# A recomputed order table for the same operations, and other forms for some filling matmuls

## The chip, the cores and the metric

The kernel runs on one core of one Trainium2 chip. The metric is the device time of the run in microseconds, lower is better. Times before and after come from runs on a chip; the profile is one further execution of the same program, taken by the hardware profiler.

## What is computed

The reference runs two layers one after the other on an input of 4 batches, 6272 time steps and 256 channels. The first is a gated recurrence over time, the second a gated long convolution over time, with a projection before and after it. Cut to what matters:

```python
sig = 1 / (1 + exp(-f_logit))
f = lower_bound + (1 - lower_bound) * sig
for t in range(S):                      # S = 6272
    h = f[:, t] * h + (1 - f[:, t]) * x[:, t]
    y[:, t] = h
proj = y @ w_proj                       # 256 -> 768
x1, x2, x3 = split(proj, 3)             # 256 channels each
x2c = irfft(rfft(x2, axis=time) * rfft(filter_fft, axis=time))
out = (x1 * x2c * x3) @ w_out           # 256 -> 256
```

Inputs and output are fp32.

## The kernel before

The kernel works through the four batches. Each goes through these stages, and the names are those by which the operations are called in the code (`kind`), in the trace lines and in the prediction.

- **Recurrence** (`hgrn`): 13 chunks of 512 time steps (the last of 128). SP loads `f_logit` into FL and `x` into XT, three buffers each (L301). ACT takes the sigmoid of FL (`sig`, L304), POOL multiplies XT by it (`u`, L306), PE transposes both in 128x128 fp32 pieces (`sT`, `uT`, L313), ACT or DVE forms the forget gate (`f`, L327 or L329), and DVE runs the scan (`scan`, L335) into the fp16 tile HA. A copy of the first 3072 steps (`wrap`, ACT or POOL) follows.
- **x2 projection** (`P`, L662): 13 groups on PE, twelve of four blocks and one short one of a single block. Each group is copied into the tile X2 by ACT or DVE (`x2`); the short copy is 128x256, the others 128x1024. All of them must be done before F1.
- **Spectrum**: 16 units. `F1` (L675) and its copy `A`; `F2` (L720); the product with the filter's spectrum Hu, two per unit, always on DVE (`prod`, L733); `slot` on POOL (L725); `I2` (L743) and its copy `Th`. SP loads Hu (`H`, L710) into three buffers in turn; such a load waits for the products that last read its buffer.
- **Gate** (`x13`, L362): x1 and x3, copied by ACT or DVE (`xs`), multiplied on POOL (`z`, L378).
- **Output** (`phase_o`): `I1` (L776), the gating product `y` on DVE (L782), `proj` (L794), the copy `o` into one of three buffers osb by ACT or DVE, and the store by SP (L804).

Stages of neighbouring batches overlap: the recurrence of the next batch runs beside the spectrum and output of the current one.

Before batch 0 the filter is transformed once (`prepare`): 13 blocks are loaded (L568), cast to fp32r by ACT, DVE or POOL (`fr`) into two buffers in turn, rotated on PE (`rot`, L579), copied (`f2`), and then transformed by `FF1` (L604, copy `afs`) and `FF2` (L622, copy `hw`, stores `hst`, L630). Between the rotations PE runs 32 blocks of filling matmuls (`warm`, L550) whose results nobody reads. Tables of sines and cosines are made on the way.

The order of all this is not found at run time. Every operation is first entered into a list with the engines that may run it. The long text ORDER then holds one entry of three characters for each of the 2438 operations: its number, the engine that it runs on, and the PSUM bank that it uses. The program is emitted in exactly this order, so that each engine, and SP's queue of DMA issues too, works through its own part of the table in sequence; what an operation must wait for on other engines is done with semaphores. Decoding is short:

```python
word = a * 4096 + b * 64 + c
yield word // 64, self.ENGINES[word // 8 % 8], word % 8
```

Of the kernel before, what the change touches and what calls it, by code (L numbers as in the profile page):

```python
# [10 lines left out]
F32R = mybir.dt.float32r  # L11
# [10 lines left out]
S = 6272  # L22
D = 256
M = 128
Q = 49
# [33 lines left out]
class Plan:  # L59
# [58 lines left out]
    "BLgAAYBBgAOYABIA6QA8gACIBGgAsRBQgBagAwSA7YBVgAPIBkgAqTBfgAtUBpgA2VBCYAeWERgA9ABDQBugA+SBEAAgXBHYAfUBAKAQABzg"  # L118
    "ArVBFIBMYA3WBIUARIB4gAmXBRAAVYBNQAYYAnWBJEESgA5XA/CBSWBPAApSBbYBOAADgAyTBUGA0SAzTBWABcQEfgAvSBTOBeABlYBXSBdA"
    "AUIAkWEggBgIBKEAxXBYCA4QBZCAdREtgASABhWETAAjUBqYBmQEugAoVBnIBvYAuSBjOAiTAFgBrUBiGATIBwSBoABsMB0YEVWBtEB5IAcX"  # L120
    "BxCAWIAEYB6QByCB1UEUYB8IB7AAlXB3EB2MAhSEXOB/QEhACKSCAICBUCIWCCEEiYEWQCJGEaRCLCCTUEcJE7gEvACNWEYICESCDYCOGCMY"
    "EbREwYCUEEjQEdJE8gEkWElAEoXCFCCaUEmOFJgEpQAZYCbEExRFKgEqHCRSCQgCcUCGgErICSCClWAHACVYCWSEzBCdMEyQE9ACmOCeYE2R"
    "E0IE3UE4BFXgE+YE/VFYgCXCCjWE5MCsQCkGCYgCfSFLACPgFBNCoWCHgCnYC1UCtACpOFMYCgCFAQFERFCIC2EFFWFlgFGBFNXCZgC3SB9Y"
    "FmgFHOFPHFOUFZACuQC4KFSVDJWFQMFUFFxgFTSCrgAIAFbTFygCvAFVKC6UChgFdDCwYCigCxQC5YC7EFaYDHSCyIDKGC+UFnADAWC/MDSQ"
    "AJADIKFcUDBGFgVFeMDCYDMSFoYFiFF9gDDWAKAAbVDEODTADQUALAFhQFzADLYDRMFpRF+gDbWFjIFrBCqgF0YDZUAMAFqRDaEFtQFsJDNC"
    "FuUGJgF1VGKgDcGDUYDVSF3NCzgDdYDeWDWCFvIF2RFwMF/ADkSF5VDlCF4JF6QGAYGVgF7FA1UGWgDtSDfGF8IDiUDuCGBRDrWDjEAaYGDJ"
    "GCSGLAGFTDmYGEKD0UE1AGhgGMYGGQGHDGNRDsOGigDnSGPJC0gC8gDwWD1EGIIDvYGXAGORFRYD2UGQJGRQGYYD3EGtgEeAD9UGTIC9gFDA"
    "GSRD+EGZQGUJGugD/UD4YGbADGgFWYDFgGjAGaQDXgEAMAGgGdRGcIGeUGkYGfBGlVDoCGgMD5QGnFEGSDqgDxODPgGvAEBYGmUDYgGwYEHC"
    "DOgGpVMvgGoMAXYEISE6YGrFDzgGqWM9gFIYEJCGxXGyVGsOJsUD6ADygEKYFfYEPSANAEsYGzPECQEQCG0NEZYELWFkYG1VEMGG2SJtTEnY"
    "G3NG4KJxVB+YEDAENgHCWG5gNLgJuEM+gHGQJvDD7gEEgJzFJwYHOSDpgHHIHDGEFgHEUM/AMwgHPKHAWEOgHFEHKQHBOJySD8gJ2THLIJ0C"  # L130
    "G8UMxAG6WNAYG9EHIQJ4DHSUHJIHQSHTEJ1YNNAG+UHegHRKG7GHMQG/EJ3SHNIHlgJ7TJ5CDggJ8WDhgJ6YMzXJ9LJ+GNMgHUUM1HHWQJ/Y"
    "HVEKASHXIHYWKBTMyYHZGHfUKDLHmQKCCHiMKFWHsgHaSKHGHhMKGXKEYM0VKIHKKWHoIHbCKLUKJYM4XKMGHcSM2NKPQNZgKNEHzgKQWKRA"
    "KOYM5UHdKKSGNBVM6HHpIKUQKTYH8SKWANCWM7MIEgNDFH6QHgYHnYH9CNOYKVXH7INGVKXHKZUNngNIFHjSNagNEOKbEHtQKYYHkCH0UHvI"
    "KaXNbAKeWHuYHwIHqSKcHKgGKfQH1YHrCH2MKdYH+WILgKjRH/GIASKhIKkUKlBH3MHxWKiYIBCIFQHyOKmEICSNHVNpAKnYIDKIgWNogKoU"
    "NJNISgIhGKpSKtTKqEIIIH4WKrCKuVH5GKsYIHIKyUKzSKvDIMWKwFIGYK0MIZgM8YIiQK1CIOOINYK3TKxYIjANPVNQUIPONRFK4SIJQK6C"
    "NSMIqgK5DITVIUYNqYIKANUXIWNNVSNWHN1gNdTIkQNXKNfDIaWK2YIlAIQTIVNImQNcYIRDK8SIdOIxgInAIXTIcOK9VIYDLBXK7YIoQK/F"
    "IrTI4gIpIK+CLCWIuLN3AIbYLGVLAYIeQLDHItLLHSLEGNeULJCLFYJGWI/gNgMLIFNiTN2gIfANjSIsYLKYNrVJHGNkLIyQNlKNtFJITNKY"
    "IvWIzYJJDI1ILLVIwGLMSLQTI0ILNFI5WLOCJKUI7OLSDJQgLPYNsRJLEODgLRQOEgNuJI2SN4YLTANwWI3CI8OJAUM3ALVQNyGNxRJDMJXg"
    "LUYLWSLaTLYCNzJJMWI6YLXALbVJNGLZYN5SJCMN6QN7CJOWLfRJPOLcDJegN+ULhBN8IOPgI9SLdFOQgOAEJRWLeYJYQI+CJUOLgVOFAJSY"
    "LkUJBYJESJTONYAOGYN/XLiFJbIOHWJlgLmEObgJFCJVUOcgJaIOJGJfRJZYJWELjYLlTJiJLpWLnDLqQN0AJcULoYJhJLsAOITLrGJnYSJS"  # L140
    "JdEJgYOBPNmYJmQORALtYOLWJpIJjUONGOngOSYOMXSLCJoISKWJkEOogOTRSMGSOSOKLOdAJqUOUQOOPOVBOeYOXWOYTJrEOfROWIO0gOZG"
    "LuUOzgSQCLzWLvMOhBSPQOpAOgSL0OOjRLwUNvAOqYO/gSRAOaLL4WLxEOkQL5OOlBOrTLygNTYL1UOmIL6WL2EOiKL9QL7GL3gMCUPAgL+I"
    "OsSOtDOvWO1AMDMOwXPLgL/QOxGL8gO2YOuKP7gO3TMAAMEUOyPO5DMBgMHQOCAMMSMIIMFEO4WO7XPBAMGgMNKMJUVMgO9HPMgPCYO8QO6O"
    "PNAPDRMKEMRSO+INhAMWWMLgMOUN9AQJgNFYMSKPFBPEQMPEPHRPGIMTSPJBMQgQCgMbUMXOMUCPIRPOYVOAMcMPPQMYSPRAPQWPKJPTXMZC"
    "MdUPUQPSOVQSPVHVpgPWIMgWMagVSKPrQVagMeEMhOMVgPZSMfgPsIVNgMlUVbgPnWPaKPbQPoGMmMPlSPjWPmCPhUPkOPtSPiEPcIPXWPuC"
    "PpUPYGPvQMqSPqEPwIPfWPdQPgGMiUPeIVcAMnWMjEMrKSNYPxQMoGPzSPyIP3UVPYP0CP1WP4MSTQP2GP8RSVAQDWP+JSSYP5TSUVSYQP6L"
    "SWFSZRSaAP/JSXYQXTSbBSdVQYDQZQQGOQQgQEYSeSP9YQaAQATQFOSiXSfFQLYScYSjQSgCQKVQhgQBDVogQHRShYQNNSlASkHSnTSoUQIB"
    "QMNQSYSmYQRWSpDQiQSqEQTOQogQOSSrYMpgSsVQUOQPCStUSxWSvESuNQVSSzGQkISwYSyXQWCQbUS2WQlIS0HVRQQcES1YQdSVTIS3XQeC"
    "VVRVdYQpUVXJV2gS4GQfSS7QQvgS5HQsMQ2gVWWS9AS8RQgKTAXS6YS+BVeQVYOQ/SQqYTBVQjYRACS/YVfRQrMVjWTCHMsSVgIVlGRHgTDF"
    "V3gTFUMtKVqAWEgQ9WTEYTHMQwSVhJQ+GTGQVUYQmUTIATKWTJYQnEQzKQtQTMGRBUQyKQuAQ4YQ3WVrYRCETLTQ6OROgRDQVkSREAVsUQ5O"  # L150
    "WFgQxYTPVTNDQ0QTRFVmKTOYRVgRIWVuETQTQ1ARLOQ7UTSDRjQQ8ERFSRGKRkARWURKORPSRQYTTYWGATUXRlQRRKRcgTWHRJYTVWWHYRmA"
    "TZXRSKVtSTbHRMQRtgTaXRNARZMVxTRXYTXGRTQRYMTcHRdVRUATdYTeXRgNR0gVzDRaQWSgTYYV4ATfURfNTjTRbATkWReYV5YVvKR7gThE"
    "RnQMugTlDRuUTmGRhSRxMRoAToWTgHRpQRwMVyVTiYRqAV6XWTgRiKTpUSCgV8HTnYRrQTqGRsIR1STrEV0NR8WWUATtQTsYTuRR3KTvATyU"
    "V1YTwBV7VT0ERvYTzQR4KR2YTxYV/RT1AWASWggWBBV9NRyTWhgT2YMkgR5QRzDR+OT3VSEYWVYT4TT5FWCKWIUT6DT8WWKEWJVR/OT+GSDS"
    "R6AT9UR9YT7YSGKUBWVZAUCXT/ESAQWLNUDGWNTUEHWOUSBAUFYWsgSFKUGWWtgWiAWWXUAYWXVWPLWbQWYHSHRWQMW4gWjYUIGUHTSIBamX"
    "WZNanWUJDWcUWdAWkRW5gUKYapGWeMWlSWmBWoTVnYaoHarQXEgWnKWpVVwYatAUQWXFgWqDUaQUROWuAULSasUWvYUMKUSWauEW6AWwUWrN"
    "UNSWyEUTGWDYUbIWxVWRYW0UUOCUkWUUgW7YWzNUVQW2EUPgW1SUWIXGAXQgW8TXRgUcUW+DWMYW3KXHYW9QXARW/IUXSXCBXcgUdEXBRUlO"
    "XIQUYCUfUXDJUuWV+AUZgUmSXKAXdgUgMUegXSAXJRUvOXMQXTYUhUXOAXogXLJUpWUiEXNQUqOXeAXURXpgXVUUjgXPIXYVXWBUrWXfYUnC"
    "XXMXZRXaFUogXgQUsGdpgUzSXbJU4UXiAUtgU9WU0KWaAUwQXqAXrYU1SUxAU5MViAXhQUygU+OU2CXkRdqgVCUXjIXmBXlWdrAXsXXtSXwT"
    "XnOU6QeFgXuHU3gWfAd4gXvKU7AU/WVDMXyDXxSVHQVAGdtTXzKYAUdsYdvLVBgeGgX+WYBEd3gYmgX2SX/OYYgYfgYKUVIIX3KYIWavYYEQ"  # L160
    "YJGaqYX6SYLEawWX7KYFAaxXX8UeHAYMQYGSYNAX9EX4QYHKYCUX5AX0SYDMayGa1QX1Ca2Ra3IduWazHa4JYOUa0YYQSdwOYPEYUQa6XYVA"
    "a5YYRKYSUa7WYTEa/Qa9OYZRbBAYWTY0VYbJa8HbAQa+YY1FbEXYXLbFRbCAYgVYcJbHBbDYYnTbGHY2QYiNYtgbJSYaYY3AbIYbKXYjNbOV"
    "bLCdyQYhYbMHYdRd0IY+gbQFYkWYeBYqLYoYbNYbPVYlGY4QYpLbTSbRFYuWbVCbSYbUUZFgY5AYwObYVYvYY6SbWEYxOYrQbaFbXYY7CbZW"
    "YsIY/UZMgdxYbbGeTgY8SbdXd5AY9KYyQZBMbfHZaSZHYYzAZAYbeWbcYZCMbiXZbCZGQZNUZTgbgGZIIZDSbkHZJIbjWZECZOYbhYdzXblG"
    "ZcSZPMd7QbmYZdCbnRZQMboWbpBZKSd6Yd9Ad1PZrgZUUZLCZkgbsRbqGZWMZeSbuBZgWbrYZfCZRQZXMbtUZVYZSAbxSZhOZygbyTbvEd8V"
# [24 lines left out]
def kernel(  # L190
# [193 lines left out]
    def prepare(tmp):  # L384
# [162 lines left out]
        def warm(e, p):  # L547
            half = iden[:].bitcast(F16)
            for i in range(4):
                nc.tensor.matmul(PS[:, p, 0:256], half[:, 0:128], half, start=True, stop=True)  # L550
        for i in range(WARM):
            op("warm", {"PE": 0.435}, warm, r=["iden"], take=1)
# [313 lines left out]
```

## Time and profile before

| | us |
|---|---|
| Median of 3 runs | 487.26 |
| Lowest and highest of them | 486.27, 487.69 |
| Profiled execution | 488.11 |
| Its span, first to last instruction | 486.3 |
| PE busy in the span | 467.5 |
| DVE busy | 425.1 |
| ACT busy | 417.5 |
| POOL busy | 295.0 |

The profiled execution lies 0.85 us above the median, so a difference that is worked out in its trace is applied to the median. Busy times of PE are modelled at the ends of matmuls, which overlap in the pipeline: a row of several matmuls is read by the distance from one start to the next, not by the mean of one. The first P of each batch starts at 79.8, 183.1, 292.0 and 396.8 us.

### The profile page before, as it was taken

To read this page: it belongs to the slowest core of one execution; us is meant where nothing else is said; L and a number is where in the kernel's file an instruction comes from. 1 tells how busy PE (TensorE), PEld (TensorE's weight loads), DVE (VectorE), ACT (ScalarE), POOL (GpSimd) and SP (SyncE) were. 2 spreads that over 40 slices of the span, in tenths; PEclk is the share of its full clock that TensorE was granted. 3 is DMA by queue.
4 is the path that set the end of the run, shared out by engine and by line. 5 is a ranking of instruction groups with operands and counts; after the bars stand their busy time and mean duration, and the time that the engine had idled before them with its cause. 6 is when DMAs were issued, how large, how long until landed. Compare 5 with 4: busy or idle time off the path is not lost.

```text
span 486.3 us, 13200 instructions
## 1 busy us (share of the span) xinstructions
PE 467.5 (96%) x5257; PEld 374.3 (77%) x5257; DVE 425.1 (87%) x454; ACT 417.5 (86%) x613; POOL 295.0 (61%) x305
## 2 busy tenths in 40 slices
PE   7999999999999999999999999999999999999895
PEld 6878878777777989777778889766788997676684
DVE  8769897699999997798999985999989978999873
ACT  4989989899999885989999887999998975999654
POOL 7677686686869430686888523667797432655600
PEclk9999999999999999999999999999999999999998
DMA  8979888775678898179667999256788870365167
GB/s 329 402 249 343 288 288 266 275 233 165 182 237 260 284 356 306 40 218 261 197 207 260 343 315 324 54 166 219 253 273 295 344 273 2 107 218 157 52 250 282
DMA packets 41725, 116.39 MB, mean 239 GB/s; under 512 B 4384, under 2 KB 6304, under 8 KB 41664
## 3 DMA queue, kind: packets, MB, share of 16 engines
q1 hardware_dynamic: 41664, 115.56, 70.9%
q8 instruction: 41, 0.67, 0.5%
q14 instruction: 20, 0.16, 0.1%
HBM read 84.54 MB, written 31.00 MB: 238 GB/s over the span
## 4 chain that ended last, share of the span: by engine, by line
PE 73%; ACT 10%; DMA 6%; DVE 4%; issue 4%; POOL 2%; SPq 0%; ACTq 0%; DVEq 0%; POOLq 0%
PE PS L362 15%; PE PS L313 15%; PE PS L743 8%; PE PS L794 7%; PE PS L662 7%; PE PS L720 6%; PE PS L675 6%; DMA out_dram<-osb 5%; PE PS L776 3%; PE PS L604 3%; ACT f L273 2%; ACT osb L275 2%; DVE X L278 1%; ACT Th L273 1%; PE PS L622 1%
## 5 line engine op out<-in xcount | busy, mean ns | idle before, releaser
L378 POOL TENSOR_TENSOR zt<-x1s,x3s 128x490 f16<-128x490 f32 (+1 forms) x104 | 125.6, 1216 | 74.9 <-ACT x3s L273 31.7
L733 DVE TENSOR_TENSOR PP<-PS,Hu 98x1008 f16<-98x1008 f32 x128 | 147.4, 1198 | 5.3 <-PE PS L720 2.3
L306 POOL TENSOR_TENSOR XT<-XT,FL 128x1024 f32<-128x1024 f32 (+1 forms) x52 | 116.9, 2249 | 55.9 <-ACT FL L304 24.1
L335 DVE TENSOR_TENSOR_SCAN HA<-fTs,HA,PS 128x512 f16<-128x512 f32 (+1 forms) x96 | 113.8, 1204 | 7.1 <-PE PS L313 3.9
L362 PE MATMUL PS<-HA,W 128*128 128x490 f16 (+1 forms) x416 | 107.5, 368 | 0.0
L782 DVE TENSOR_TENSOR ys<-PS,zt 128x1024 fp32r<-128x1024 f32 (+1 forms) x52 | 58.8, 1151 | 7.0 <-PE PS L776 4.8
L313 PE MATMUL PS<-iden,XT 128*128 128x128 f32 x392 | 61.2, 276 | 2.8 <-POOL XT L306 1.1
L327 ACT ACTIVATE fTs<-PS,nomc 128x512 f32<-128x512 f32 (+1 forms) x87 | 58.7, 676 | 5.7 <-PE PS L313 3.5
L275 ACT ACTIVATE osb<-PS 128x1024 f32<-128x1024 f32 (+1 forms) x49 | 48.0, 988 | 16.9 <-PE PS L794 10.2
L313 PE MATMUL PS<-iden,FL 128*128 128x128 f32 x392 | 60.6, 275 | 0.5 <-DVE PP L733 0.4
L273 ACT CAST HA<-PS 128x1024 f16<-128x1024 f32 x56 | 56.7, 1024 | 4.6 <-PE PS L675 4.3
L743 PEld LDWEIGHTS <-PP 98*128 98x128 f16 x1024 | 50.0, 98 | 12.2 <-issue 3.2
L275 ACT ACTIVATE x1s<-PS 128x490 f32<-128x490 f32 (+1 forms) x97 | 57.2, 594 | 2.5 <-PE PS L362 0.7
L794 PE MATMUL PS<-Wo,ys 128*128 128x256 f32 x392 | 57.6, 291 | 1.4 <-ACT osb L275 0.7
L273 ACT COPY x3s<-PS 128x490 f32<-128x490 f32 (+1 forms) x94 | 53.7, 577 | 5.9 <-PE PS L362 4.6
L304 ACT ACTIVATE FL<-FL 128x1024 f32<-128x1024 f32 (+1 forms) x52 | 53.7, 1033 | 0.5 <-DMA FL<-in_f_logit_dram 0.4
L313 PEld LDWEIGHTS PS<-iden,XT 128*128 128x128 f32 x392 | 44.6, 140 | 11.2 <-issue 3.0
L794 PEld LDWEIGHTS PS<-Wo,ys 128*128 128x128 f32 x392 | 49.3, 188 | 4.7 <-ACT osb L275 1.7
L362 PEld LDWEIGHTS <-W 128*128 128x128 f16 x416 | 34.6, 98 | 23.3 <-issue 6.4
L743 PE MATMUL PS<-VA,PP 98*128 98x98 f16 x512 | 52.1, 207 | 0.4 <-DVE PP L733 0.2
L273 ACT CAST Th<-PS 128x784 f16<-128x784 f32 x60 | 49.8, 831 | 2.9 <-PE PS L743 2.3
L743 PE MATMUL PS<-VB,PP 98*128 98x98 f16 x512 | 51.9, 207 | 0.0
(111 smaller groups left out, 692.0 us busy)
## 6 DMA issues: line engine op xcount, KB each, us to landing
Hu<-H SPq DMA_DIRECT2D x64, 392.0 KB
FL<-in_f_logit_dram SPq DMA_DIRECT2D x48, 512.0 KB
XT<-in_x_dram SPq DMA_DIRECT2D x48, 512.0 KB
out_dram<-osb SPq DMA_DIRECT2D x48, 512.0 KB
X<-in_moe_filter_fft_dram SPq DMA_DIRECT2D x9, 512.0 KB
H<-Hu SPq DMA_DIRECT2D x16, 196.0 KB
H<-Hu SPq DMA_DIRECT2D x16, 128.0 KB
Hu<-in_moe_filter_fft_dram SPq DMA_DIRECT2D x2, 512.0 KB
```

Of the source, the lines that this page charges most:

```text
L273: nc.scalar.copy(dst, src)
L275: nc.scalar.activation(dst, src, AF.Copy, scale=scale)
L306: op("u", {"POOL": 0.1 + 0.553 * nb}, lambda e, xt=xt, ft=ft: nc.gpsimd.tensor_tensor(xt, xt, ft, op=AOP.mult), r=[("ft", k)], w=[("xt", k)])
L313: nc.tensor.transpose(PS[:, p, j:128 * nb:nb], src[:, j, cols], iden[:])
L327: nc.scalar.activation(fT, PS[:, p, 0:n], AF.Identity, scale=by, bias=1.0)
L335: nc.vector.tensor_tensor_scan(h, fT, PS[:, p, 0:n], init, op0=AOP.mult, op1=AOP.add),
L362: nc.tensor.matmul(PS[:, p, 0:n], W13[:, kh, js], HA[:, HB[kh] + t0:HB[kh] + t0 + n], start=(kh == 0), stop=(kh == 1))
L378: nc.gpsimd.tensor_tensor(late["zt"][:, jb, :, m0:m0 + nm], xs(0), xs(1), op=AOP.mult),
L733: nc.vector.tensor_tensor(PP[:TB, k, o, :, :, 1:64], px.unsqueeze(1).broadcast_to([TB, 2, UE, 63]), hh[:, :, :, 1:64], op=AOP.mult)
L743: nc.tensor.matmul(PS[:, ib + o, pr * TB:(pr + 1) * TB], PP[:TB, k, o, n, 2 * pr:2 * pr + 2, :], v[:TB], start=(n == 0), stop=(n == 1))
L782: nc.vector.tensor_tensor(late["ys"][:, yk, :, 0:rn * 128], PS[:, cb:cb + 2, 0:rn * 128], late["zt"][:].rearrange("p k r m -> p k (r m)") ...
L794: nc.tensor.matmul(po[:, i, :], late["ys"][:, yk, kh, i * 128:(i + 1) * 128], Wo[:, kh, :], start=(kh == 0), stop=(kh == 1))
```

## The change

There are two edits. The first replaces the whole text ORDER by another for the same 2438 operations (same operands, same dependences, same engines allowed). Decoded and set side by side, 122 operations run on another engine than before; most of them are copies that both ACT and DVE may do, and `wrap`, which ACT or POOL may do. Many PSUM banks differ. PE's list keeps its overall sequence, with swaps of neighbours over a few places. SP's list has loads, stores and H loads in other places, among them the load of lower_bound (wcol), several of the filter blocks, and the first H load of batch 2.

The second edit gives 15 of the 32 filling blocks a form by their number: 12 of these differ from the wide f16 matmul of before. They are full and half transposes in fp32 and fp32r, and matmuls in fp32r; all blocks but four are now also entered as readers of `rot`, a 128x256 copy of the identity that DVE makes at the start.

```diff
 ORDER = (
-    "BLgAAYBBgAOYABIA6QA8gACIBGgAsRBQgBagAwSA7YBVgAPIBkgAqTBfgAtUBpgA2VBCYAeWERgA9ABDQBugA+SBEAAgXBHYAfUBAKAQABzg"
...
+    "A8gAAYBBgAOYABIAxQBLgACIBGgA6RBVgBQgAeSBfgBagAnTAPIAmUADgA9YAdVBpgBCAAtWA2XBkgBDQA+SERgApUA/CBHYBMIAsVBACAvW"
...
 )
...
-        def warm(e, p):
+        def warm(e, p, i):
             half = iden[:].bitcast(F16)
-            for i in range(4):
-                nc.tensor.matmul(PS[:, p, 0:256], half[:, 0:128], half, start=True, stop=True)
+            ro = rot[:, 0:128]
+            full, wide = PS[:, p, 0:128], PS[:, p, 0:256]
+            for j in range(4):
+                if i in (0, 1):
+                    nc.tensor.matmul(wide, half[:, 0:128], half, start=True, stop=True)
+                elif i in (2, 8):
+                    nc.tensor.transpose(full, iden[:], iden[:])
+                elif i in (3, 9):
+                    nc.tensor.transpose(PS[:, p, 0:64], iden[0:64], iden[0:64, 0:64])
+                elif i in (4, 10):
+                    nc.tensor.transpose(full.bitcast(F32R), ro, ro)
+                elif i == 5 and j < 2:
+                    nc.tensor.matmul(full, ro, ro, start=True, stop=True)
+                elif i in (6, 12):
+                    nc.tensor.matmul(wide, ro, rot[:], start=True, stop=True)
+                elif i in (7, 13):
+                    nc.tensor.transpose(PS[:, p, 0:64].bitcast(F32R), ro[0:64], rot[0:64, 0:64])
+                elif i in (14,):
+                    nc.tensor.transpose(PS[0:64, p, 0:128], iden[:, 0:64], iden[:])
+                else:
+                    nc.tensor.matmul(wide, half[:, 0:128], half, start=True, stop=True)
+        pos = (49, 58, 41, 44, 47, 31, 34, 46, 42, 51, 36, 32, 56, 52, 48)
         for i in range(WARM):
-            op("warm", {"PE": 0.435}, warm, r=["iden"], take=1)
+            i = pos.index(i + 27) if i + 27 in pos else 99
+            op("warm", {"PE": 0.435}, lambda e, p, i=i: warm(e, p, i), r=["iden", "rot"] if i > 3 else ["iden"], take=1)
```

## The prediction

> **What bounds the kernel now.** I read the page first (busy shares, slices), then the stretches by stage, then the chain of waits in order of time, then single groups and timelines where the new table differs from the old one.
>
> ```profile
> span 486.3 us, 13200 instructions
> PE 467.5 (96%) x5257; PEld 374.3 (77%) x5257; DVE 425.1 (87%) x454; ACT 417.5 (86%) x613; POOL 295.0 (61%) x305
> ```
>
> PE has a record for 467.5 of 486.3 us; the 18.8 us without one are nearly all that an order can win (ends of matmuls are modelled, so short gaps hide behind them). The stretches say where those gaps lie; columns are length, then busy us of PE, PEld, DVE, ACT, POOL, granted clock, DMA share, GB/s.
>
> ```profile
> 0.00:12.00 12.00, 9.42 (x62) 7.38 (x63) 9.60 (x30) 5.17 (x6) 8.91 (x23) 1.00 0.85 328
> 12.00:26.00 14.00, 13.32 (x113) 11.55 (x111) 9.45 (x23) 13.97 (x23) 9.71 (x12) 1.00 1.03 402
> 26.00:80.00 54.00, 52.11 (x410) 43.36 (x411) 46.87 (x50) 48.83 (x74) 40.64 (x47) 1.00 0.85 280
> ...
> 278.00:285.00 7.00, 6.32 (x88) 5.73 (x87) 5.69 (x6) 5.10 (x8) 3.84 (x3) 1.00 1.01 345
> 285.00:292.00 7.00, 6.08 (x63) 5.18 (x62) 6.48 (x7) 6.82 (x10) 0.00 (x0) 1.00 0.94 305
> ...
> 310.00:396.00 86.00, 85.49 (x1050) 67.89 (x1049) 83.27 (x82) 79.84 (x122) 59.85 (x56) 1.00 0.74 249
> ...
> 411.00:460.00 49.00, 47.43 (x610) 31.78 (x611) 44.68 (x48) 44.58 (x70) 31.27 (x40) 1.00 0.44 133
> 460.00:486.30 26.30, 19.94 (x293) 17.59 (x286) 14.93 (x13) 12.67 (x13) 0.20 (x1) 0.94 0.62 246
> ```
>
> So PE's gaps are 3.3 us before 26 us (DMA at its full share there), 1.9 in the first recurrence (ACT busy 48.8 of 54), 1.6 between 278 and 292, 1.6 in the last batch's spectrum, 6.4 at the end. From 310 to 396 only 0.5 is left. The chain names the releaser at these places:
>
> ```profile
> 25.50 0.70 DVE f L278
> 26.25 2.18 PE PS L604 x16
> ...
> 277.85 7.14 DMA out_dram<-osb
> 285.10 1.03 ACT osb L275
> ...
> 478.31 3.33 DMA out_dram<-osb
> ```
>
> The filter's transform (L604) starts at 26.25 behind a copy; a store took 7.14 us from issue to landing among loads, but 3.33 in the idle end.
>
> **The change, part by part.** Decoded, both tables hold the same 2438 operations; 122 change engine, many change bank, and PE's order differs by a few places almost everywhere. Work is not removed.
>
> *Start (L568, L579, L604).* Thirteen blocks of the filter arrive 1.28 us apart (the queue's issues at 16.39, 17.68, 18.96 step by that), are cast (POOL 1.04, ACT 1.05, DVE 0.68), rotated on PE (0.72) and copied (0.60 to 0.69), with two cast buffers in turn. New: DVE casts block 3 ahead of its second table instead of POOL; POOL's padding (1.85+0.23) goes from before its first cast to after its fourth; SP issues wcol (1 KB) before the last five blocks, and the short block 12 before 10 and 11. I followed the new lists with these durations: POOL ends the padding at 17.1, casts 8 until 18.15, 9 from 18.9 (its buffer), 10 from 20.4 (0.4 of om in between), 11 until 22.45; ACT's cast of 12 ends at 22.8, its copy of 8 at 23.4, which frees the bank for the rotation of 11 (to 24.1); ACT's last copy ends at 25.1. FF1 at 25.2, against 26.25: **-1.0**. wcol costs between 0 and one slot of 1.28 us; in the trace it kept a slot in the issue row (13.84, next at 15.12), but 1 KB cannot fill one: I take 0.2, inside the -1.0. Bounds: +0.5 to -2.
>
> *First recurrence (26 to 80).* ACT: four f copies come from DVE and two go (+2x0.68), hw +1x1.03, afs -5x0.60, wrap -1x0.62: -1.2 us. DVE: -2x0.74 -1.22 +5x0.68 = +0.7, against 7 us of DVE gap. As ACT is the fuller, half of its relief: **-0.6** (bounds 0 and -1.9, PE's gap).
>
> *Short x2 copy.* The 128x256 copy costs more than the four times larger one:
>
> ```profile
> L273 ACT CAST X<-PS 128x1024 f16<-128x1024 f32 x26 | 25.9, 1037 | 14.9 <-PE PS L662 14.1 <-DVE osb L280 0.8
> L273 ACT CAST X<-PS 128x256 f16<-128x256 f32 x2 | 2.6, 1304 | 0.3 <-PE PS L662 0.3
> L278 DVE CAST X<-PS 128x256 f16<-128x256 f32 x2 | 2.6, 1299 | 1.3 <-PE PS L662 1.3
> ```
>
> In batch 3 it was DVE's last before the first F1 (at 409.53). New: it is fourth of four x2 copies on DVE, ACT's nine end the phase, and proj waits beside them. P takes 0.88 per block, so P, four x13 and that proj end 13.4 us after P's start, against 12.75 measured; but then only four F1 and four x13 (3.4) come before the first F2, against 4.85 before. F2, which starts DVE's run of 32 products (1.2 each, DVE 44.7 of 49 busy), comes 0.7 earlier; DVE's list behind it loses one Th (0.97) and gains one xs (0.6). **-0.8** (bounds +0.7, -1.6).
>
> *Stores and loads.* SP's list at the end of batch 1 had (by operation number) load 1501, store 1310, loads 1512 and 1513, stores 1315 and 1320; now 1310 stands ahead of 1501, and both 1315 and 1320 ahead of 1513. The Trainium skill (SBUF — State Buffer, "The DMA setup-cost knee") fits one transfer as 2 us plus bytes over 436 GB/s: 3.2 us for 512 KB, like the 3.33 at the end; by it alone a store's place would not matter. The trace's 7.14 does: 3.8 more, or three slots of 1.28. By the rule this part is 0; by the row one slot less, -1.28 where PE lost 1.6. I take **-1.0**, and -0.2 for the like change at 167 to 183, where PE's gap was 0.5: **-1.2**. Past what SP moves: the first H load of batch 2 (L710) now stands before the last twelve loads for batch 2's recurrence and waits there for unit 13's products; those end near 248.2 in the trace, where the load before it issued at 248.33. Cost 0 under that cover.
>
> *Batch 2.* DVE loses two f, two o, gains one x2: about -2.7 us. PE gap only 0.5: **-0.3**.
>
> *End.* One 512 KB output copy and the last short one go from ACT to DVE. ACT did all thirteen, held by stores (idle 1.20 and 1.00 before two of them). DVE has twelve y of 1.23, one short one, and room. The last proj now follows I1 and y (0.9 us more on PE's side), but PE ended at 480.6, before ACT's 482.1. **-0.4** (bounds +0.9, -1.5).
>
> *Fills.* Twelve of 32 blocks change form; the first eight stay wide f16.
>
> ```profile
> 1.36 5.23 PE L550 MATMUL PS<-iden 128*128 128x256 f16 x28 [1.36 <-POOL iden masks.py:199]
> 13.69 1.91 PE L550 MATMUL PS<-iden 128*128 128x256 f16 x16
> ```
>
> A block is 4x0.12 = 0.48. Full transposes run 8 in 0.87, so 0.44; fp32r matmuls of 256 columns 16 in 2.18, so 0.54; the half transposes and fp32r forms of 128 are not shown: between 0 and 0.54 a block. Sum between -5.8 and +0.7 on PE, all beside the casts: **0**. Their read of rot (ready at 1.8) starts after two blocks: 0. Without that cover a fill delays one rotation by its length.
> A rule speaks against them: the skill (TensorE: Matmul & The Clock Gate, "Part 4: PE-mode transpose") says that transposes do not count as PE activity for the clock. The fence shows the slow start: 187 ns a fill, then 119 (the clock column reads 1.00 in both, so pitch must tell). By the rule the stage could fall back to slow rotations: 13 blocks x 0.48, about +5 with two buffers in turn. By the trace, 33 of 71 matmuls between 57 and 66 us were transposes, still at 0.109. I take 0: the rotations between the fills, and three of the twelve blocks, stay matmuls.
>
> **Sum:** -1.0 -0.6 -0.8 -1.2 -0.3 -0.4 = -4.3. A new order meets new waits: outside start and end PE's gaps are 9.2 us over 434; I charge a tenth, +1.0. Net -3.3. The profiled execution took 488.11 (span 486.3 plus 1.8); the three runs' median 487.26 is 0.85 lower, so the forecast is 484.0.
>
> **Rivals.** (a) *PE's queue takes it all back*: gaps are only 0.5 in 86 us in the middle; a stage that starts earlier may wait later for products or loads. For: DVE at 97% of 310 to 396. Against: start and end are not PE-bound. 487.
> (b) *Slower by the clock*: place, 9 to 25 us; price up to +5; decides where fills between rotations step by over 0.2 us. 484.0+5 = 489.
> (c) *The H load blocks SP*: if unit 13's products end later than the XT load before it by over 6 us (the next load was at 254.78), loads of batch 2 slip by the rest; 3 us late gives 487 to 490. Against: 0 wait in the old times.
>
> **Numbers.** The likeliest case has 0.74, (a) 0.13, (b) 0.07, (c) 0.06. About 0.3% (1.5 us) is what a measurement of this kernel can tell from no change. The likeliest alone spans 479.5 to 486 (its bounds in part); with the others and a larger gain of the recomputed order, 478.5 to 488.5. Faster 0.73, same 0.13, slower 0.14.
>
> **What would show it.** L604 first at about 25.2; P at about 78; fills stepping 0.11 to 0.14; no store of over 6 us on the chain near 278 and PE's gap of 278 to 292 below 1; F2 of batch 3 some 16.9 us after its P; the tail some 26 us. Wrong if P is not earlier than 79.5, or if PE's gaps from 80 to 460 exceed 9 us.

## The result and the profile after

The new kernel takes 488.07 us (median of 20 runs, 486.8 to 489.67) against 486.92 us of the kernel before (20 runs on the same chip). The ratio is 1.0021, 95% interval [1.0006, 1.0036]: a little slower, by about 1 us. The forecast was 484.0, faster. It was wrong in sign. The profiled execution took 488.59 us (span 486.5), the one before 488.11 (486.3); these two lie 0.5 and 1.2 us above their medians.

The page of the new kernel opens like the old one: PE's busy time has even grown.

```profile
span 486.5 us, 13197 instructions
PE 469.2 (96%) x5257; PEld 375.6 (77%) x5257; DVE 422.1 (87%) x453; ACT 418.5 (86%) x612; POOL 296.8 (61%) x307
```

The stretches, with the columns of before (length, busy us of PE, PEld, DVE, ACT, POOL, clock, DMA share, GB/s), show where:

```profile
0.00:12.00 12.00, 10.66 (x72) 8.65 (x72) 9.11 (x32) 5.71 (x7) 6.47 (x19) 1.00 0.86 332
12.00:26.00 14.00, 12.23 (x100) 10.47 (x99) 9.65 (x19) 10.52 (x16) 9.81 (x11) 1.00 0.99 383
26.00:80.00 54.00, 51.33 (x400) 42.30 (x400) 46.41 (x51) 48.09 (x73) 42.04 (x51) 1.00 0.83 273
278.00:285.00 7.00, 7.00 (x106) 6.29 (x105) 7.00 (x7) 6.72 (x10) 3.21 (x2) 1.00 0.89 302
285.00:292.00 7.00, 6.81 (x67) 5.76 (x65) 6.72 (x8) 5.34 (x8) 0.73 (x1) 1.00 0.98 311
411.00:460.00 49.00, 47.55 (x620) 31.81 (x619) 43.32 (x47) 43.92 (x69) 32.25 (x40) 1.00 0.44 133
460.00:486.30 26.30, 19.92 (x278) 17.23 (x272) 16.40 (x15) 11.17 (x11) 0.00 (x0) 0.97 0.62 246
```

PE's gap between 278 and 292 fell from 1.6 to 0.2 us; over 80 to 460 it fell from 7.3 to 5.0. But between 12 and 26 us ACT, which had been full (13.97 of 14), is busy only 10.52, and PE is down from 13.32 to 12.23. The start got worse, the middle better. Marks taken from the first matmul of each kind make it a sum (us from one mark to the next; FF1 is L604 before, L625 after; P is L662 and L683, I1 is L776 and L797; the P of the four batches starts at 79.65, 183.04, 291.87 and 396.62 before, a little earlier than in the list ahead of the prediction):

| from, to | before | after | difference |
|---|---|---|---|
| start, FF1 | 26.25 | 28.74 | +2.49 |
| FF1, P of batch 0 | 53.40 | 53.80 | +0.40 |
| P of batch 0, P of 1 | 103.39 | 102.28 | -1.11 |
| P of batch 1, P of 2 | 108.83 | 107.20 | -1.63 |
| P of batch 2, P of 3 | 104.75 | 104.51 | -0.24 |
| P of batch 3, its first I1 | 63.15 | 62.81 | -0.34 |
| first I1, end of span | 26.53 | 27.16 | +0.63 |
| sum | 486.30 | 486.50 | +0.20 |

The table sets one execution beside one other, so it adds up to 0.20 and not to the 1.15 between the medians. Its rows behind the start sum to -2.29.

The chain of waits of the new kernel leads back from FF1 through two places (start, length, what):

```profile
15.42 1.87 POOL f L579
...
17.31 0.05 ACT f L273
...
24.57 1.25 DVE FTr L517
...
26.34 0.69 DVE f L278
...
27.05 1.64 ACT f L273 x4
...
28.74 1.33 PE PS L625 x9
```

L579 is POOL's padding of f2, L517 the scaling of the small table FTr. Neither was on the chain before. The timelines of the engines (start, length, engine, line, operation, and in brackets the idle time ahead of it and its releaser) show what each did:

```profile
17.31 0.71 DVE L278 CAST f<-PS 128x512 fp32r<-128x512 f32 x1 [2.81 <-POOL f L579]
...
17.31 1.18 ACT L273 CAST f<-PS 128x512 fp32r<-128x512 f32 x2 [1.95 <-POOL f L579]
...
23.97 2.38 POOL L306 TENSOR_TENSOR XT<-XT,FL 128x1024 f32<-128x1024 f32 x1
...
24.47 1.95 DVE L517 TENSOR_SCALAR FTr<-PP,cols 128x98 fp32r<-128x98 f32 x1
...
27.05 1.63 ACT L273 CAST f<-PS 128x512 fp32r<-128x512 f32 x4 [2.14 <-DVE f L278]
```

First, at 17.31 both DVE and ACT resume at once; they had stood 2.81 and 1.95 us for the padding. In the code the padding writes the columns between the blocks of f2 (and its last 16), the copies write the blocks; the table of operations gives it a tag of its own, f2e, so an order may put it anywhere ahead of FF1. The program on the chip nevertheless makes the copies wait, though the padding gives them no value: both write the same stretch of one tile. In the old kernel the padding was over at 5.88 us, ahead of the first copy at 8.40:

```profile
3.87 1.85 POOL L558 CAST f<-iden 128x1920 fp32r<-128x1920 f32 x1
```

Second, DVE's scaling of FTr takes 1.95 us. In the old kernel it had taken 0.26, and its timeline has it just ahead of POOL's first multiply instead of inside it:

```profile
23.24 0.26 DVE L517 TENSOR_SCALAR FTr<-PP,cols 128x98 fp32r<-128x98 f32 x1
...
23.67 2.37 POOL L306 TENSOR_TENSOR XT<-XT,FL 128x1024 f32<-128x1024 f32 x1
```

So the theory to be tested (theory A in the expectations): the padding's place and the scaling beside the multiply cost the start some 3.5 us against the forecast, and the rest of the table is a gain. The rivals: other things pace the start (rival B there); a later stage takes the start's gain back (rival C); the fills do it; the gain in the middle is not what the prediction said it is.

### The profile page after: what moved, and what is told of

Same layout as the page of the kernel before. It is cut to its first block, busy times and chain, and to the rows that moved or that the text cites. A ratio compares the mean times of both kernels' runs of the same rounds, so it can differ in the third digit from the quotient of the medians.

```text
span 486.5 us, 13197 instructions
## 1 busy us (share of the span) xinstructions
PE 469.2 (96%) x5257; PEld 375.6 (77%) x5257; DVE 422.1 (87%) x453; ACT 418.5 (86%) x612; POOL 296.8 (61%) x307
## 4 chain that ended last, share of the span: by engine, by line
PE 75%; ACT 8%; DVE 5%; POOL 4%; DMA 4%; issue 3%; SPq 0%; ACTq 0%; DVEq 0%; POOLq 0%
PE PS L362 15%; PE PS L313 14%; PE PS L683 9%; PE PS L764 8%; PE PS L815 7%; PE PS L741 6%; PE PS L696 6%; PE PS L797 4%; POOL XT L306 2%; DMA out_dram<-osb 2%; PE PS L625 2%; DVE HA L335 2%; ACT osb L275 2%; DMA XT<-in_x_dram 1%; ACT Th L273 1%
## 5 line engine op out<-in xcount | busy, mean ns | idle before, releaser
L362 PE MATMUL PS<-HA,W 128*128 128x490 f16 (+1 forms) x416 | 107.0, 367 | 0.3 <-DVE HA L335 0.2
L327 ACT ACTIVATE fTs<-PS,nomc 128x512 f32<-128x512 f32 (+1 forms) x91 | 61.2, 675 | 8.0 <-PE PS L313 5.1
L273 ACT COPY x3s<-PS 128x490 f32<-128x490 f32 (+1 forms) x92 | 52.7, 574 | 5.1 <-PE PS L362 3.6
```

Of the source, the lines that this page charges most:

```text
L273: nc.scalar.copy(dst, src)
L327: nc.scalar.activation(fT, PS[:, p, 0:n], AF.Identity, scale=by, bias=1.0)
L362: nc.tensor.matmul(PS[:, p, 0:n], W13[:, kh, js], HA[:, HB[kh] + t0:HB[kh] + t0 + n], start=(kh == 0), stop=(kh == 1))
```

## Experiments on the start

Edits are given as the decoded lists of one engine. A cast of filter block n is written "fr n". In the first four kernels the text of ORDER takes two lines less, so line numbers behind it are lower by two there.

**The padding alone** (on POOL's list):

```diff
 iden, iota, fr 0,
+pad f2,
 fr 2, fr 4, fr 6,
-pad f2,
 fr 8, fr 9, wcol, fr 10, fr 11, u 0
```

> The new table with one operation moved: POOL's padding of f2 comes right behind POOL's first cast of a filter block (about 5.6 to 7.6 us) instead of behind its fourth (15.42 to 17.41). Theory A (the padding is one half of the lost start: the f2 copies on ACT and DVE, idle from 15.3 and 14.5 us until 17.31, wait for it): the copies no longer wait at 17.31, the filter's transform (L625) starts at 26.7 to 27.3 instead of 28.74, batch 0's P at 80.5 to 81.5 instead of 82.54, and the time is 1 to 2 us under the new kernel's, so 0.998 to 1.000 of the kernel before. Rival B (the padding only stands beside the wait; SP's arrival of blocks or the rotations pace the start): the transform stays at 28.5 or later. Rival C (the start is taken back later, because the recurrence of batch 0 or the loads behind it set P): the transform comes earlier by 1.5 or more but P of batch 0 and the end do not move, ratio 1.002.

Measured: 486.44 us, ratio 0.9988 [0.9971, 1.0005]; FF1 at 27.17, P of batch 0 at 80.44. The copies no longer wait for the padding. FF1 gains 1.57 and the end keeps it (ratio down by 0.0033, 1.6 us). But another operation of DVE now stood beside the multiply, the cast of D1r that takes 0.28 us elsewhere:

```profile
23.35 2.37 POOL L304 TENSOR_TENSOR XT<-XT,FL 128x1024 f32<-128x1024 f32 x1 [0.23 <-ACT f L271]
...
23.70 2.17 DVE L512 CAST D1r<-PP 128x256 fp32r<-128x256 f32 x1
```

**The scaling alone** (on DVE's list; the two scalings of FTr need only the first sine):

```diff
 args, fr 3, args,
+FTr, FTr 2,
 f2, f2, f2, f2, f2,
-FTr,
 f2, f2, f2,
-FTr 2,
 f2, D1r, f2
```

> The new table with two operations moved: DVE's two scalings of the small table FTr (L517; 0.87 us at 21.88 and 1.95 us at 24.47 in the new kernel) stand right behind DVE's trigonometric arguments and the first sine, ahead of DVE's f2 copies, where DVE was idle from 14.5 to 17.31. The padding stays late. Theory A (the second scaling, slowed from 0.26 to 1.95 us beside POOL's multiply of XT, is the other half of the lost start, since ACT's f2 copies wait 2.14 us for the DVE copy behind it): the two scalings take 0.3 to 1 us each, the transform starts at 26.5 to 27.3 instead of 28.74, and the time is 1 to 2 us under the new kernel's, 0.998 to 1.000 of the kernel before. Rival B (ACT or the rotations are as late without it): the transform stays within 0.5 of 28.74.

Measured: 487.14 us, 1.0002 [0.9984, 1.0020]; FF1 at 26.81, P of batch 0 at 80.87. FF1 gains 1.93 with the padding still late. The ratio lies just above the range expected, and the gain of 0.9 us at the end is by itself within the two intervals.

**Both:**

> The new table with both moves: the padding behind POOL's first cast and DVE's two scalings of FTr ahead of its f2 copies. Theory A (two separate causes that add up): the transform starts at 25.0 to 25.7, which is what the prediction had (25.2), batch 0's P at 78.8 to 79.8, and the time is 3 to 3.5 us under the new kernel's, 0.994 to 0.997 of the kernel before. Rival B (one of them hides the other, or block arrivals are next): the transform at 26.2 to 27, 0.997 to 0.999. Rival C (the gain is taken back behind the start): transform early, ratio 1.000 or more.

Measured: 484.59 us, ratio 0.9956 [0.9938, 0.9974]; FF1 at 26.04, P of batch 0 at 79.50, span 482.5. At the end the two moves add up: 3.2 us less than the new kernel, where they gave 1.6 and 0.9 alone; the difference lies within the intervals, of some 0.9 us each way. FF1 gains 2.70, less than the two apart, and does not reach 25.2. The chain shows what is next:

```profile
10.83 10.16 DMA X<-in_moe_filter_fft_dram
...
21.14 1.05 POOL afs L281
...
25.38 0.61 ACT f L271
...
26.04 1.68 PE PS L623 x12
```

It now runs back to the loading of the filter's blocks. By the ratio this is 2.1 us under the kernel before, where the forecast for the change had 3.3.

A single reading of FF1 can be off by most of a microsecond: this kernel and six below whose edits leave the order of its start alone have it at 25.26 to 26.79, and P of batch 0 at 79.08 to 80.62 (a seventh, told of under the multiply, came later for a reason of its own). With the start of the new kernel three profiles have FF1 at 27.95 to 28.74, so the two groups stay apart.

**The old start with the new rest, and the reverse:**

```diff
-ORDER = new[0:2438]
+ORDER = old[0:122] + (new without these)
```

> The old table up to the first matmul group of the filter's transform (its first 122 entries), and behind it the new table's order. Theory A (the start alone made the forecast wrong; everything behind it is worth what the milestones show, 79.65 to 478.79 before against 82.54 to 480.1): the transform starts at 26.2, batch 0's P at 79.5 to 80.2, and the time is 2 to 2.9 us under the new kernel's, 0.995 to 0.998 of the kernel before. Rival C (the rest of the new table was gaining only because it started late, having slack to take up): ratio 1.000 to 1.002 in spite of the early transform.

Measured: 485.03 us, 0.9954 [0.9939, 0.9969]; FF1 at 26.36, P of batch 0 at 80.70, half a microsecond later than expected; the ratio is as expected.

```diff
-ORDER = new[0:2438]
+ORDER = new[0:250] + (old without these)
```

> The new table's first 250 entries (all of the start and the first blocks of the recurrence), and behind them the old table's order. Theory A (start and the rest add up): the transform at 28.7, batch 0's P at 82.3 to 83, from there on the old kernel's distances (316.97 from batch 0's P to batch 3's P, 399.14 to the last I1), the end 2.5 to 3 us behind the kernel before, ratio 1.005 to 1.007. Rival C (the old order has slack behind the start that takes the delay up): ratio 1.000 to 1.003.

Measured: 490.13 us, 1.0058 [1.0032, 1.0083]; FF1 at 28.55, P of batch 0 at 83.32, span 488.5. The new start costs the old order some 2.8 us, the old start saves the new order 3.3 us. No later stage takes it up: rival C is out for the start as a whole.

**The padding put late in the old table:**

```diff
 iden, iota,
-pad f2,
 fr 1, fr 2, fr 3, FTs, rest, fr 6,
+pad f2,
 fr 8, fr 9, fr 10, fr 11
```

> The old table with one operation moved: the padding of f2 behind POOL's fourth cast of a filter block, where the new table has it. Theory A (this alone costs most of 2 us): the f2 copies on ACT and DVE stand until 16.5 to 17.5, the transform starts at 27.5 to 28.5 instead of 26.25, P of batch 0 1 to 2 us later, ratio 1.002 to 1.004; DVE's first scalings (L482, 3.45 us beside the padding) fall to some 1.8. Rival B (only the new order is sensitive to it): transform within 0.5 of 26.25, ratio 0.999 to 1.001. The distances behind the start also give a second reading of the old order: 103.4, 108.8 and 104.75 from P to P.

Measured: 490.55 us, 1.0063 [1.0044, 1.0083]; FF1 at 30.07, P of batch 0 at 83.66. One operation of 2 us, moved in the old kernel, costs 3.1 us at the end, more than expected. The timeline of ACT shows the wait, and the stretches a second loss: the granted clock.

```profile
14.89 2.04 POOL L558 CAST f<-iden 128x1920 fp32r<-128x1920 f32 x1
...
16.88 0.64 POOL L560 CAST f<-iden 128x16 fp32r<-128x16 f32 x1
...
16.96 1.22 ACT L273 CAST f<-PS 128x512 fp32r<-128x512 f32 x2 [2.91 <-POOL f L558]
```

ACT resumes at the end of L558, the gaps between the blocks (16.93), while L560, the last 16 columns of the same tile, runs on to 17.52. So the wait is for the operation whose columns lie among those of the copies, not for every writer of the tile.

```profile
12.00:20.00 8.00, 5.79 (x42) 4.90 (x41) 6.89 (x13) 5.09 (x9) 6.33 (x7) 0.86 1.03 406
20.00:26.00 6.00, 6.00 (x50) 5.29 (x49) 2.23 (x5) 5.13 (x8) 2.07 (x3) 0.90 1.03 394
```

**Is it the multiply that slows DVE?** The first try moved the multiply behind the last f2 copies in the new table's text:

```diff
-... FTr 2 (DVE), ..., u 0 (POOL), f2, f2, f2, f2, FF1
+... FTr 2 (DVE), ..., f2, f2, f2, f2, u 0 (POOL), FF1
```

> The new table with one operation moved: POOL's first multiply of XT (L306) is emitted behind the last f2 copies instead of ahead of them, so that it no longer starts at 23.97 beside DVE's second scaling of FTr, which keeps its place. The padding stays late. Theory A (the scaling is held by that multiply: 1.95 us here and 2.17 us for the cast of D1r in the first variant, each ending within 0.2 us of the multiply's end, against 0.26 to 0.4 elsewhere): the scaling takes 0.3 to 0.9 us, the transform starts at 26.8 to 27.6 instead of 28.74; batch 0's first u comes up to 2 us later, so P may gain less, and the time is between 1.0003 and 0.998 of the kernel before. Rival B (the scaling waits for something of its own or is slow by its place): 1.5 us or more again and the transform at 28.5.

Measured: 488.48 us, 1.0023 [1.0000, 1.0047]; FF1 at 27.95. The edit failed as an experiment: POOL's own list is the same, nothing made POOL wait, and the multiply began at 24.13, near the 23.97 of the new kernel. It is in effect a second measurement of the new kernel, and agrees with the first. But in this execution the scaling was over by then (0.34 us), and the cast of D1r stood beside the multiply: 2.17 us. The second try starts from the kernel with both moves and puts the scaling there on purpose, with the padding early:

```diff
-FTr, FTr 2, f2, ..., D1r, f2
+FTr, f2, ..., D1r, FTr 2, f2
```

> The kernel with both moves at the start, with DVE's second scaling of FTr put behind the cast of D1r, ahead of the last f2 copy on DVE, so that it falls in the time of POOL's first multiply of XT (23.70 to 26.13 in the kernel without this edit). The padding is early. Theory A (an operation of DVE that reads and writes SBUF stands until the multiply's end): the scaling takes 1.5 to 2.3 us and ends within 0.2 us of the multiply, the transform starts at 27.0 to 27.8 instead of 26.04. Rival B (that was the padding's lateness or the place, not the multiply): 0.2 to 0.9 us, transform at 26.0 to 26.5.

Measured: 487.14 us, 1.0008 [0.9991, 1.0026]; FF1 at 27.61, P of batch 0 at 83.01.

```profile
23.73 0.28 DVE L514 CAST D1r<-PP 128x256 fp32r<-128x256 f32 x1
...
23.81 2.43 POOL L306 TENSOR_TENSOR XT<-XT,FL 128x1024 f32<-128x1024 f32 x1 [0.23 <-ACT f L273]
...
23.93 2.38 DVE L517 TENSOR_SCALAR FTr<-PP,cols 128x98 fp32r<-128x98 f32 x1
```

The scaling ends at 26.31, 0.07 us behind the multiply's end at 26.24. In the new kernel it was 26.42 against 26.35, in the first variant D1r 25.87 against 25.72, in the run ahead 26.65 against 26.50. D1r, with 256 columns, ends 0.14 to 0.15 us behind the multiply, the scaling, with 98, only 0.07. So the DVE operation does not run slower; it stands until POOL is done. Copies from PSUM beside the same multiply keep their time (0.71 us at 24.64 in the kernel with both moves, inside its multiply of 23.70 to 26.13). The Trainium skill (SBUF — State Buffer, "SBUF: two separate sides") states this rule: VectorE in some modes and GpSimd share a pair of SBUF ports by an exclusive lock, and whichever starts second is blocked for the other's whole instruction. The rows agree with it where DVE is second; by my estimate, shared bandwidth would have given an operation of 0.28 us perhaps twice its time, 0.6 us, not 2.2. Where POOL is second, 0.20 us of D1r are left at its start and the multiply grows by only 0.06 us (2.37 to 2.43), so the rows do not show that side of the rule in full.

The timing is a close race. In the kernel with both moves D1r began 0.08 us ahead of the multiply, in another kernel with the same start (the one with late loads, below) 0.06 us behind it:

```profile
23.62 0.28 DVE L512 CAST D1r<-PP 128x256 fp32r<-128x256 f32 x1
...
23.70 2.43 POOL L304 TENSOR_TENSOR XT<-XT,FL 128x1024 f32<-128x1024 f32 x1 [0.23 <-ACT f L271]
```

```profile
23.49 2.37 POOL L306 TENSOR_TENSOR XT<-XT,FL 128x1024 f32<-128x1024 f32 x1 [0.23 <-ACT f L273]
...
23.55 2.46 DVE L514 CAST D1r<-PP 128x256 fp32r<-128x256 f32 x1
```

There FF1 came at 27.30 instead of 26.04. That speaks for moving D1r ahead of the copies too; the last run below tries it.

**The fills:**

```diff
-                if i in (0, 1): ... elif i in (2, 8): ... (nine forms)
+                nc.tensor.matmul(wide, half[:, 0:128], half, start=True, stop=True)
```

> The kernel with both moves at the start, and all 32 fill blocks as four wide f16 matmuls, as before. Theory A (the forms of the fills are worth nothing, as the prediction has it): transform at 26.0, batch 0's P at 79.5, ratio 0.9956, clock 0.995 or more. Rival B (the other forms cost or spare PE time in the start, or change the clock): the transform or P of batch 0 differ by over 0.3, or the granted clock over the first 30 us falls.

Measured: 485.25 us, 0.9960 [0.9938, 0.9982]; FF1 at 25.75, P of batch 0 at 79.61, clock 1.00 over the first 40 us. The forms are worth nothing that can be measured (to about 1 us), and do not lower the clock.

## Experiments on the middle and the end

**Three stores of batch 1 put back** (on SP's list, from the kernel with both moves):

```diff
-store 1310, load 1501, load 1512, store 1315, store 1320, load 1513
+load 1501, store 1310, load 1512, load 1513, store 1315, store 1320
```

> The kernel with both moves at the start, and on SP's list three output stores of batch 1 back behind the loads they stood behind in the old table (1310 behind load 1501, 1315 and 1320 behind load 1513). Theory A (the prediction's step of -1.0: a late store holds an output buffer and with it an ACT copy and PE): from batch 1's P to batch 2's P 108.5 to 108.9 us, as before (108.83), against 107.2 to 107.5 in the new kernel and its four variants, and the end 1.0 to 1.6 later than without this edit, ratio 0.998 to 0.999. Rival B (the other moves between those phases, engines and copies, made the gain): 107.2 to 107.6, ratio 0.9956.

Measured: 485.34 us, 0.9955 [0.9934, 0.9975]; from P of batch 1 to P of batch 2 107.69 us. By the prediction, an earlier store was to free the ACT copy for which PE stood near 285. Before, PE stood 0.76 us there; with the stores back behind the loads, it stands 0.18 (the line before, then this run):

```profile
286.26 0.63 PE L313 MATMUL PS<-iden,XT 128*128 128x128 f32 x4 [0.76 <-ACT osb L275]
```

```profile
284.26 0.63 PE L313 MATMUL PS<-iden,XT 128*128 128x128 f32 x4 [0.18 <-ACT osb L275]
```

The new kernel and the kernel with both moves have 0.18 too, and the latter's stage is 107.53 in its own profile. So the prediction's cause for its -1.0 falls: the gap stays closed without it. The time alone, with an interval of about 1 us each way, could not have told.

**SP's whole list of that stretch put back:** (entries 1240 to 1560, about 40 loads and stores)

> The kernel with both moves at the start, and SP's list from entry 1240 to 1560 in the old table's relative order: stores 1310, 1315, 1320 back, loads 1898, 1912 ahead of where they are, 1911 behind 1926, store 1340 last; all other engines as in the new table. Theory A (the gain between batch 1's P and batch 2's P sits in SP's list as a whole): 108.3 to 108.9 us there, PE gaps of 0.5 and more near 95 and 102 us behind P as before. Rival B (it sits in the order and the engines of the copies; SP's list is worth nothing): 107.2 to 107.7, ratio 0.9956.

Measured: 487.34 us, 1.0006 [0.9982, 1.0029]; 110.96 us from P to P. That stage is slower than in either kernel, and for reasons of its own: in this mixture a load of the filter's spectrum comes late, DVE's products stand for it, and PE for them; and then the granted clock falls.

```profile
244.88 2.32 DVE L754 TENSOR_TENSOR PP<-PS,Hu 98x1008 f16<-98x1008 f32 x2 [1.78 <-DMA Hu<-H]
```

```profile
245.00:250.00 5.00, 3.41 (x39) 2.76 (x39) 5.00 (x5) 2.95 (x5) 2.96 (x7) 0.80 0.96 255
250.00:255.00 5.00, 5.00 (x45) 3.43 (x44) 3.56 (x4) 4.28 (x8) 4.20 (x4) 0.86 0.14 52
```

PE does 39 and 45 matmuls in these stretches; in the kernel with both moves it does 62 and 62 at a clock of 1.00. The old kernel has no such gap on DVE at that place. So the 3.4 us by which this stage is longer than with both moves are a late load and a slower clock together; the run does not separate them, and does not tell where the old kernel lost.

**Three recurrence loads alone put back** (1898 ahead of 1925, 1912 ahead of 1340, 1911 behind 1926):

```diff
-store 1330, load 1911, load 1925, store 1335, store 1340, load 1898, load 1912, load 1926
+store 1330, load 1898, load 1925, store 1335, load 1912, store 1340, load 1926, load 1911
```

> The kernel with both moves at the start, and three loads for batch 2's recurrence back in the old table's places on SP's list (1898 ahead of 1925, 1912 ahead of 1340, 1911 behind 1926); stores and H loads as in the new table. In the old kernel PE stood 0.63 us for POOL's XT and 0.76 us for an ACT copy held by a store at 278 and 285. Theory A (these loads stand in the stores' way): from batch 1's P to batch 2's 108 to 108.8 us and PE gaps of 0.3 to 0.8 near 95 and 102 us behind P. Rival B (the engines of the copies and PE's order make the gain): 107.2 to 107.7.

Measured: 485.60 us, 0.9984 [0.9959, 1.0009]; 107.49 us from P to P. Not the loads either.

**The old order from entry 1300, and from entry 1430, to the end:**

```diff
-ORDER = both_moves[0:2438]
+ORDER = both_moves[0:1300] + (old without these)      # and the same with 1430
```

> The kernel with both moves at the start up to entry 1300 of its table (some 60 us behind batch 1's P), and from there the old order to the end. Theory A (the gain between batch 1's P and batch 2's lies in the recurrence and output behind that point): 107.9 to 108.8 us from P to P there, then 104.75 to 105.15 to batch 3's P, last batch 62.7 to 63.2 to its first I1, tail 26.5 to 26.9; ratio 0.998 to 1.000. Rival B (it lies ahead of that point): 107.2 to 107.6.

> As the run ahead of it, with the cut at entry 1430 (just behind batch 1's first I1, some 80 us behind its P). Theory A (the stores and loads among batch 1's output, at 90 to 107 us behind its P, make the gain): 107.9 to 108.8 us from P to P. Rival B (it lies between 60 and 80 us, in the products and the first outputs): 107.2 to 107.6 here, and more in the run ahead of it.

Measured: 485.68 us, 0.9973 [0.9960, 0.9986], with 108.12 us from P to P; and 484.76 us, 0.9962 [0.9947, 0.9977], with 107.78. Other readings of the old order are 108.83, 107.96 and 108.06 (the old kernel, the new start with the old rest, the late padding); the new order gives 107.19 to 107.22 in eight profiles and 107.0 to 108.1 in all. So the gain of this stage is about 0.9 us rather than the 1.6 of the two first profiles. By these two cuts it lies behind entry 1300, more than half of it behind 1430, among batch 1's output; but each is one reading, and the new order's own readings spread as widely. Neither the three stores nor the three loads alone carry it, and what does stays open.

**The old end** (all thirteen output copies of the last batch on ACT, last proj ahead of the last but one's y):

```diff
-ORDER = both_moves[0:2438]
+ORDER = both_moves[0:2373] + (old without these)
```

> The kernel with both moves at the start (padding and FTr), and from the last batch's first I1 on the old table's order: all thirteen output copies on ACT, the last proj ahead of the last but one's y, banks as before. Theory A (the new order of the output stage costs 0.6 us: from the first I1 to the end of the span 26.53 us before, 27.16 in the new kernel and 27.0 to 27.2 in the four runs behind it): 26.4 to 26.7 from the first I1 to the end here, span 481.9 instead of 482.5, time 0.3 to 0.7 us less, ratio 0.994 to 0.995. Rival B (the output stage is paced by its stores, which take what they take: 6.4 MB): 27.0 to 27.2 again, ratio 0.9956.

Measured: 484.97 us, 0.9956 [0.9936, 0.9976]; 26.73 us from the first I1 to the end. That is 0.34 less than without the edit, at the edge of what was expected, and not seen in the time. Over all profiles the old end takes 26.5 to 27.4 (28.3 in one), the new end 27.0 to 27.7. The stage ends on stores in either order, as the new kernel's chain shows; its last short copy, now on DVE, waits for one too:

```profile
464.78 5.00 DMA out_dram<-osb
...
473.87 4.10 DMA out_dram<-osb
...
479.12 2.72 DMA out_dram<-osb
...
481.94 0.42 DVE osb L280
```

**Candidates that should beat both kernels.** The first: both moves, the old end, wcol's load behind the last filter block, and POOL's use of it behind its first multiply.

```diff
 SP:   ..., block 6,
-wcol,
 block 9, block 8, load, block 12, block 10, block 11,
+wcol,
 POOL: fr 8, fr 9,
-wcol,
 fr 10, fr 11, u 0
+wcol
```

> The new table with the padding behind POOL's first cast, both FTr scalings ahead of DVE's f2 copies, the old order from the last batch's first I1 on, and wcol's load behind the last filter block (POOL's use of it behind its first multiply). Theory A (the start is now paced by the blocks' arrival, and wcol takes a part of a slot of 1.28 us): the transform at 25.0 to 25.8, the span 481 to 482.5, ratio 0.993 to 0.9955, faster than both kernels. Rival B (wcol costs nothing, and the recurrence takes up what the start gives): transform at 26.0, ratio 0.9956.

Measured: 485.32 us, 0.9958 [0.9940, 0.9976]; FF1 at 25.31, but P of batch 0 at 80.60. FF1 comes 0.7 earlier than with both moves, but from FF1 to P it takes 55.3 us instead of 53.5, and the end is the same. The chain of that stage runs through two loads of XT, of 6.68 and 6.92 us, where that of the kernel with both moves stays nearly all on PE. The profiled execution lies 1.5 us above the median of this kernel, so how far wcol's place has to do with it is not shown.

The second: both moves, D1r beside FTr ahead of the copies, and the old end.

```diff
 args, fr 3, args,
-FTr, FTr 2, f2, ..., D1r, f2
+FTr, FTr 2, D1r, f2, ..., f2
```

> The new table with the padding behind POOL's first cast, both scalings of FTr and the cast of D1r ahead of DVE's f2 copies, and the old order from the last batch's first I1 on. Theory A (in the profiles with both moves the cast of D1r, 0.28 us long, began 0.06 to 0.08 us ahead of POOL's multiply in seven, and 0.06 us behind it in late_loads, where it took 2.46 us; its place is a close race that some executions lose, so their times spread to 488 and 489): with no SBUF-only operation of DVE left beside that multiply, the transform starts at 25.2 to 26.2, the span is 481.5 to 483, the ratio 0.993 to 0.9955, and the spread of the times is narrower. Rival B (the race is rare or costs nothing at the end): ratio 0.9956 and the same spread.

Measured: 484.86 us, ratio 0.9966 [0.9953, 0.9979], slightly outside what was expected; span 481.6, the shortest of all profiles, but of this kernel's fastest run; FF1 at 26.03, P of batch 0 at 79.40. The times spread over 3.0 us (483.34 to 486.38, 17 runs), against 6.2 (12 runs) in the kernel that lost the race in its profile, but 2.1 (11 runs) in the kernel with both moves; so the narrower spread is not shown. It beats the kernel before by 0.2 to 0.5%, and by the two ratios the new kernel by 0.55%; it is no better than both moves alone (0.9956), so moving D1r brought no gain that shows.

## Why the prediction was wrong, step by step

- **Start, -1.0 (measured +2.49): the step that failed.** The forecast and the measured start lie 3.5 us apart, most of the 4.5 between the forecast's -3.3 and the measured +1.15. Its dates for POOL were good: the padding's end was put at 17.1 and came at 17.41. What failed is the sentence that moved the padding "after its fourth" cast and then followed only POOL. It never asked who waits for the padding. ACT and DVE did, 1.95 and 2.81 us. The second half is that every duration was taken as fixed: FTr's scaling has 0.26 in the old profile, and 1.95 once the new order put it beside POOL's multiply. Each was shown by moving it alone and by moving both, the padding also by the reverse in the old table, the scaling by putting it back beside the multiply. With both repaired FF1 is at 26.04, and at 25.26 to 26.79 in kernels with the same start, so the forecast's 25.2 stands at the early end even so; the chain there runs back to the arrival of the blocks. The bound of +0.5 was far too tight for a step that moves an operation behind which two engines queue.
- **First recurrence, -0.6 (measured +0.40):** from FF1 to P of batch 0 the repaired kernels take 53.3 to 54.1 in most profiles, the old order 53.4 and 53.6. No gain shows; relief on ACT did not become time.
- **Short x2 copy, -0.8:** the first half of the mechanism was right: F2 of batch 3 came 16.72 us after its P (forecast 16.9, before 17.70). Of this, 0.34 was left at the first I1, so the term was about twice too large. What took up the rest was not tried; the 32 products of DVE behind F2 are the likely place.
- **Stores and loads, -1.2:** the gap near 278 did close, and P to P of batch 1 lost 1.63, so the number looked right. The cause was not: with the stores put back the gap stayed closed. The size over several profiles is 0.9. From P of batch 0 to P of batch 1 the forecast had -0.2, the profile -1.11; what made that gain was not tried.
- **Batch 2, -0.3 (measured -0.24):** the number agrees; that DVE's relief made it was not tried.
- **End, -0.4 (measured +0.63):** wrong in sign in these two profiles; the order costs 0.3 in the direct trial, within the spread of that stage.
- **Fills, 0:** right, and rival (b) is refuted in its cause. But the clock did fall elsewhere, see below.
- **The charge of +1.0 for new waits** was spread over the middle, where PE's gaps went down. The new waits were in the start, which the prediction had left out of the charge. Without the start the forecast has -2.3, charge included, and the table -2.29; the old start with the new rest came out 2.2 us under the kernel before. As the parts do not agree one by one, that is luck.

The prediction named "P not earlier than 79.5" as its own refutation, and P came at 82.54.

## What to carry to other kernels

When an operation is moved later, list everything that writes or reads the same stretch of its tile, not only the operations that need its values: here columns that lay between the others' columns were enough for a wait. A duration from the old profile holds only beside the same neighbours; for a small VectorE operation from SBUF to SBUF, look at what GpSimd runs at its new time, and place it where GpSimd is idle or VectorE waits anyway. And when a stage's gap closes as forecast, put the claimed cause back by itself before believing it: here the gap stayed closed.

## What the runs showed of the hardware

- An operation of DVE with SBUF on both sides (0.28 us) that begins while POOL multiplies two SBUF tiles ends 0.06 to 0.15 us after the multiply, having taken 1.95 to 2.46 us, in six profiles; begun 0.06 to 0.08 us ahead of it, it keeps its 0.28 us and the multiply takes 2.43 to 2.45 instead of 2.37. POOL's casts do the same for their shorter time: FTr's first scaling in the new kernel runs from 21.88 to 22.75, beside a cast of POOL that ends at 22.68.
- A hole in PE's work of a microsecond or two can cost as much again by the clock, in some executions. The stretches of the run with the scaling beside the multiply, and behind them those of the kernel with both moves:

```profile
26.00:30.00 4.00, 2.39 (x17) 2.40 (x17) 1.99 (x4) 2.67 (x4) 1.66 (x2) 0.88 0.68 270
30.00:34.00 4.00, 4.00 (x24) 3.34 (x23) 2.17 (x4) 2.14 (x3) 3.25 (x5) 0.69 0.21 54
```

```profile
26.00:30.00 4.00, 3.96 (x32) 3.76 (x34) 2.18 (x4) 3.32 (x5) 3.12 (x5) 1.00 0.66 260
30.00:34.00 4.00, 4.00 (x36) 3.57 (x34) 4.00 (x5) 3.93 (x6) 4.00 (x3) 1.00 0.79 249
```

With FF1 1.57 us later, P of batch 0 is 3.51 later: between 30 and 34 us PE does 24 matmuls instead of 36 at a granted clock of 0.69. Three of seventeen runs show the dip at this place, behind holes of 1.99, 2.07 and 2.08 us just ahead of FF1 (the moved multiply, the scaling beside the multiply, the late loads); the late padding shows it behind one of 2.21 us at 15 us. The padding alone, with a hole of 1.98 us, kept 1.00, and so did the new kernel with 1.60. But in the run with SP's old list the clock fell behind a hole of 1.14 us and one of 0.46 soon after. So the length of one hole does not decide it alone, and what does was not tried.
